# Attention and a feed-forward layer on one core: the sixth product of each output stage split into seven small ones

## The chip, the cores and the metric

The kernel runs on one core of a Trainium2 chip. The core has five engines that run side by side, each with its own queue of instructions in fixed order: TensorE (PE in the profile; PEld are its weight loads), VectorE (DVE), ScalarE (ACT), GpSimd (POOL) and SyncE (SP), which mostly issues transfers. TensorE writes into PSUM, eight banks of 512 float32 columns by 128 partitions; VectorE and ScalarE read it. The metric is device time of one execution in microseconds; lower is better.

## The reference

Eight batches of twelve heads, 448 tokens, head dimension 64. Softmax attention, then a layer with two weight matrices over all 3584 tokens, with a leaky ReLU between them:

```python
scores = scale * np.matmul(q, k.transpose(0, 1, 3, 2))
attn = np.exp(scores - max) / sum          # over the keys
x = np.matmul(attn, v)                     # to (3584, 768)
h = x @ w_in                               # (768, 2048)
g = np.maximum(0.01 * h, h)
out = g @ w_out                            # (2048, 768)
```

## The kernel before

Everything is written out by hand in one order per engine; the kernel keeps no scheduler of its own at run time, so an instruction that waits holds up all that stand behind it on its engine.

**Stages.** The tokens are cut at `cuts = [0, 640, 1152, 1664, 2176, 2688, 3072, 3584]` (line 41) into seven stages, 0 to 6. Each stage has a w_in stage (`head` and `neck` for stage 0, `hidden(i)`, line 523, after that), which makes h from x, and a w_out stage (`second(i)`, line 1134), which makes the output from h. Attention for later tokens is woven into the w_out stages: per head pair u a burst (three chunks of scores into three PSUM slots, then three exps on ScalarE), a tail (a fourth, half-sized chunk), and later rows (the weighted sum of v, divided on VectorE: a reciprocal at line 974 and a multiply at line 975), whose result x is turned by a transfer into `xT`. 48 head pairs in all.

**Fewer products.** Both matrix products are done by a scheme of Strassen's kind with seven products where eight would stand. In a w_in stage each group of seven products has 6 matmuls of 256 columns each (192 in the 384-token stage 5); two such groups run at a time, one on the two PSUM `banks`, one on two `slots`, so that a step of `hidden` has two such products, first that of the slots, then that of the banks (in the first half). A w_out stage takes two pairs of token blocks (c = 0 and 1; `spots(i)` says which) and forms for each, in `block_pair` (line 660), products of 8 matmuls with 384 columns on two banks, b and a, by turns: b, a, b, a (`early`), then b and a (`late`). After each one VectorE reads the bank into the output tiles `o1` and `o2` (`keep` copies, line 687; `join` adds, line 693). The sixth product, last of `late`, is `h[hi, one] x w_out[hi, right]` and goes into the right half of `o1`. The seventh is not formed there in stages 1 to 6: `deep(i)` (line 624) forms it for both pairs at once by a second level of the same scheme, seven products of 4 matmuls with 192 columns (line 645), one in every step of the first half of the next w_in stage, each followed by a VectorE addition of 192 columns (line 649). Its sums of h are made ahead by `deep_sums` (line 611), its sums of weights once by `mix_deep` (line 448), in w_out stage 1. In stage 6, which has no stage behind it, `deep` is interleaved with the second pair, and `closing` (line 728) ends the kernel with products cut in halves of 192 columns.

In stage 0 all seven products are formed directly, and the banks are swapped after each pair, seven being odd; in the other stages they are not swapped, six being even.

**The order of attention.** `second(i)` walks over the steps of `block_pair` (one step is two matmuls) and after each calls `place` (line 1071), a planner that keeps a model of its own: a clock `now` that a step moves on by 0.325, for each slot the time at which it comes free, and the time at which ScalarE is done. A burst is written when the three slots are due, a tail when the first slot is, rows when the exps of u are done and a slot is due. `plan` (line 1068) says how many bursts each stage writes; `cap` and `keen` say how far rows may run ahead. The assertion after the loop asks that all bursts of the plan were placed. If a tail is still owed when a w_in stage starts, the loop at line 1207 writes it ahead of the first product there:

```python
if owed_t and step == 0:
    tail()
```

**Buffers.** `xT` is a ring of twelve blocks of 128 tokens; a transposed batch of 448 tokens may run over its end, and `close_ring` (line 480) copies what ran over to the start (stage 2 alone). q, k and v are loaded two head pairs at a time from POOL's queue into `ld_pool`, two buffers each; a load may be written when `to[...]` says that the casts are far enough. Output tiles come from `o_pool`, three buffers.

Of the kernel before, what the change touches and what calls it, by code (L numbers as in the profile page):

```python
# [16 lines left out]
def kernel(  # L17
# [32 lines left out]
    ld_pool = ctx.enter_context(tc.tile_pool(name="ld", bufs=2))  # L50
    cast_pool = ctx.enter_context(tc.tile_pool(name="cast", bufs=1))
# [7 lines left out]
    o_pool = ctx.enter_context(tc.tile_pool(name="o", bufs=3))  # L59
# [43 lines left out]
    NX = 12 * P  # L103

    def place_of(t):
        return (t - cuts[5]) % NX

    OVER = max(-t % S for t in cuts if place_of(t) == 0)
# [8 lines left out]
    deep_mix = w_pool.tile([P, 3, QH, QW], BF16)  # L117
    KEEP = 4
# [20 lines left out]
    for _ in range(3):  # L139
        rooms.append(o_pool.tile([P, DM], F32, name="o").bitcast(BF16)[:, :4 * NSC * D])  # L140
# [306 lines left out]

    def mix_deep():

        t, (t2, t3, t4) = w_mix[:, 2], (deep_mix[:, x] for x in range(3))  # L450
        lo, hi, left, right = slice(0, QH), slice(QH, MH), slice(0, QW), slice(QW, NW)
        sub, add = nc.vector.tensor_sub, nc.vector.tensor_add
        for by, o, x, y in (
            (sub, t3, t[:, hi, right], t[:, lo, right]),
            (add, t2, t3, t[:, lo, left]),
            (sub, t4, t[:, hi, left], t2),
            (sub, t[:, lo, right], t[:, lo, right], t[:, lo, left]),
        ):
            by(o, x, y)
            yield  # L460
# [19 lines left out]
    def close_ring(i):  # L480

        if place_of(cuts[i]) == 0 and cuts[i] % S:
            for hp in range(KD):
                nc.vector.tensor_copy(xT[:, hp, :OVER], xT_flat[:, (hp + 1) * NX:(hp + 1) * NX + OVER])
                yield
# [37 lines left out]
    def hidden(i):  # L523
# [63 lines left out]
        more = deep(i - 1) if i > 1 else None  # L587
        for r in range(2):
            ms = [4 * r, 4 * r + 2]
            todo = [group(chains[x], ms[x]) for x in range(2)]  # L590
            for step in range(7):
                for y in range(2):
# [5 lines left out]
                    if i > 1 and (r or step) and y == 1:  # L598
                        next(more, None)
# [11 lines left out]
    def deep_sums(i):  # L611

        one, two = (ts(x[1], P) for x in spots(i)[1])
        lo, hi = slice(MH, MH + QH), slice(MH + QH, MD)
        s3, s1 = h_mix[:, :QH, 0], h_mix[:, QH:, 0]
# [8 lines left out]
    def deep(i):  # L624

        one, two = (ts(x[1], P) for x in spots(i)[1])
        lo, hi = slice(MH, MH + QH), slice(MH + QH, MD)
        s3, s1 = h_mix[:, :QH, 0], h_mix[:, QH:, 0]
        t, (t2, t3, t4) = w_mix[:, 2], (deep_mix[:, x] for x in range(3))
        left, right = slice(0, QW), slice(QW, NW)  # L630
        o = [kept[i, c] for c in range(2)]
        end = i + 1 == NR
        taken = [slots.pop(0) for _ in range(2 if end else 1)]
        b, a = (x[:, 0, :QW] for x in taken) if end else (taken[0][:, x, :QW] for x in range(2))
        for ps, first, x, w, c, cols in (
# [7 lines left out]
        ):  # L643
            for m in range(QH):
                nc.tensor.matmul(ps, x[:, m], w[:, m], start=(first and m == 0), stop=(m == QH - 1), skip_group_check=True)  # L645
            if end and c and (ps is a or cols is left):
                nc.scalar.copy(o[c][:, cols], ps)
            else:
                nc.vector.tensor_add(o[c][:, cols], o[c][:, cols], ps)  # L649
            if ps is a and first and c == 0:  # L650
                nc.vector.tensor_sub(h[:, hi, one], h[:, hi, one], s1)
            if ps is a and not first:
                store(o[0], token(i, spots(i)[1][0][1]), slice(0, NW) if end else slice(0, DM))
            if w is t4:
                if not end:
                    store(o[1], token(i, spots(i)[1][1][1]))
                slots.extend(taken)
            yield

    def block_pair(i, c):  # L660
# [12 lines left out]
        kept[i, c] = o2  # L673
# [21 lines left out]
        def early():  # L695
# [7 lines left out]
            if last:  # L703
# [9 lines left out]
            keep(o2, right, a, calm)  # L713
            yield

        def late():
# [6 lines left out]
            yield  # L723
            yield from product(a, h[:, hi, one], w_out_sb[:, hi, right])
# [3 lines left out]
        def closing():  # L728

            both = (nc.sync, nc.scalar)  # L730
            yield from product(b, s3, t3)
            join(o2, left, b)
            idle(o2[:, right], b[:, :NW])
            store(o2, t0, left, both)
            yield
            cuts2 = [(ts(x, QW), slice(NW + x * QW, NW + (x + 1) * QW)) for x in range(2)]
            for (cols, at), ps, os in zip(cuts2, (a, slots[0][:, 0]), ((o1, o2), (o2, o1))):
                yield from product(ps, h[:, lo, two], t1[:, :, cols], first=True, cols=cols)
                for o in os:
# [12 lines left out]
        if last:  # L752
            more = deep(i)
            for x, _ in enumerate(early()):
                if x == 0:
                    next(parts[0])
                yield
# [5 lines left out]
            yield from closing()  # L763
            return
        if not c:
            parts[:] = [deep_sums(i)]
# [256 lines left out]
    def fetch(n=3):  # L1023
        if to["q"] == NPE:
            return
        for x, y in enumerate(("q", "cast", "v")):
            u = to["load"][x]
            if n and u <= ahead and (u <= FAR or u - 3 < to[y]):
# [39 lines left out]
    plan = [8, 6, 6, 6, 6, 4, 0]  # L1068
# [177 lines left out]
```

## Time and profile before

| | |
|---|---|
| median of 3 runs (lowest, highest) | 377.95 us (377.93, 378.19) |
| profiled execution: time, span | 378.34 us, 376.6 us |
| TensorE busy | 369.7 us, 98% |
| VectorE, ScalarE, POOL busy | 256.9, 259.6, 191.8 us |
| granted TensorE clock | 0.999 over the span |
| matmuls of 384 columns at line 682 | 326 ns mean a record |
| matmuls of 192 columns at line 645 | 246 ns a record, 168 of them |

A matmul's record is longer than its share of the stream, since matmuls overlap: what one costs is read from the distance of starts, or from the pieces of the chain. The same holds, less so, for VectorE, whose 0.55 us operations follow one another every 0.47 us.

### The profile page before, as it was taken

How to read it: one execution, taken by the hardware profiler on the slowest of the kernel's cores; microseconds unless marked ns; L12 is line 12 of the kernel's file. 1: busy time of each engine (PE TensorE's matmuls, PEld its weight loads, DVE VectorE, ACT ScalarE, POOL GpSimd, SP SyncE). 2: the span in 40 equal slices, each digit the busy share in tenths (PEclk: the TensorE clock that was granted, in tenths of full speed). 3: DMA queues.
4: the chain of work that ended last, by engine and by line, in shares of the span. 5: the costliest groups of instructions: out<-in, count | busy, mean ns of one | idle time of the engine just before them, and what ended most of it. 6: DMA issues, size and time to landing. Idle time of an engine off the chain costs nothing.

```text
span 376.6 us, 10120 instructions
## 1 busy us (share of the span) xinstructions
PE 369.7 (98%) x4008; PEld 265.7 (71%) x4008; DVE 256.9 (68%) x558; ACT 259.6 (69%) x399; POOL 191.8 (51%) x376
## 2 busy tenths in 40 slices
PE   7999999999999999999999999999999999999996
PEld 3664658756698556996569966599665995679765
DVE  4765858778666867766676665775847775685763
ACT  5997885866768776758766587666787668636721
POOL 7985871986268989624588235792347020000000
PEclk9999999999999999999999999999999999999999
DMA  9999999999499885973869648798455740321123
GB/s 155 200 203 207 191 204 201 156 159 164 93 178 143 114 163 87 197 158 60 157 121 148 144 64 86 170 147 167 61 66 98 143 110 0 79 58 45 42 65 105
DMA packets 99600, 48.08 MB, mean 128 GB/s; under 512 B 64608, under 2 KB 96352, under 8 KB 99552
## 3 DMA queue, kind: packets, MB, share of 16 engines
q0 software_dynamic: 39600, 22.47, 44.6%
q1 hardware_dynamic: 59504, 24.50, 32.6%
q8 instruction: 31, 0.51, 0.6%
q10 hardware_dynamic: 448, 0.47, 0.4%
q14 instruction: 17, 0.14, 0.1%
HBM read 45.61 MB, written 11.01 MB: 150 GB/s over the span
## 4 chain that ended last, share of the span: by engine, by line
PE 94%; DMA 2%; DVE 1%; issue 1%; POOL 1%; ACT 1%; POOLq 0%; ACTq 0%; DVEq 0%
PE g L682 30%; PE g L548 14%; PE sc L548 14%; PE sc L322 7%; PE sc L350 6%; PE g L424 4%; PE sc L319 4%; PE sc L645 4%; PE sc L362 3%; PE g L817 2%; PE sc L343 2%; DMA w_in_mix<-in_v_dram 2%; PE g L362 1%; PE g L301 1%; PE sc L424 1%
## 5 line engine op out<-in xcount | busy, mean ns | idle before, releaser
L331 ACT ACTIVATE e<-sc 128x896 bf16<-128x896 f32 (+1 forms) x144 | 123.6, 923 | 30.7 <-PE sc L322 20.8
L682 PE MATMUL g<-w_out_sb,h 128*128 128x384 bf16 (+1 forms) x440 | 84.1, 325 | 0.0
L682 PEld LDWEIGHTS <-h 128*128 128x128 bf16 x592 | 54.4, 98 | 41.4 <-issue 11.2
L537 ACT ACTIVATE h<-c 128x512 bf16<-128x512 f32 (+1 forms) x72 | 43.1, 610 | 30.2 <-DVE c L563 12.4
L548 PEld LDWEIGHTS <-w_in_sb 128*128 128x128 bf16 x576 | 54.6, 98 | 5.7
L190 POOL COPY qkb<-fq 112x512 bf16<-112x512 bf16 x34 | 23.9, 703 | 41.6 <-DMA qkT<-qkb 32.5
L548 PEld LDWEIGHTS <-w_in_mix 128*128 128x128 bf16 x432 | 40.5, 98 | 3.7
L201 POOL COPY v<-fv 128x384 bf16<-128x384 bf16 x30 | 18.5, 617 | 43.1 <-PE sc L350 40.7
L687 DVE COPY o<-g 128x384 f32<-128x384 f32 x47 | 26.0, 553 | 13.7 <-PE g L682 13.5
L350 PE MATMUL sc<-v,e 128*128 128x65 bf16 x720 | 33.3, 193 | 0.0
L322 PE MATMUL sc<-qkT 64*128 64x448 bf16 (+1 forms) x210 | 32.8, 352 | 0.0
L350 PEld LDWEIGHTS <-e 128*128 128x128 bf16 x720 | 31.1, 98 | 1.3
L974 DVE RECIPROCAL rec<-sc 112x8 f32<-112x8 f32 x42 | 8.7, 207 | 33.6 <-PE sc L350 19.1
L975 DVE TENSOR_TENSOR x<-sc,rec 112x512 bf16<-112x512 f32 x42 | 29.0, 691 | 1.6 <-DVE rec L974 0.2
L548 PE MATMUL g<-xT,w_in_sb 128*128 128x256 bf16 (+1 forms) x216 | 28.5, 268 | 0.0
L548 PE MATMUL sc<-xT,w_in_sb 128*128 128x256 bf16 (+1 forms) x216 | 28.5, 268 | 0.0
L693 DVE TENSOR_TENSOR o<-o,g 128x384 f32<-128x384 f32 x39 | 21.4, 549 | 9.1 <-PE g L682 4.4
L343 PE MATMUL sc<-v,e 128*128 128x130 bf16 x120 | 26.5, 221 | 0.0
L649 DVE TENSOR_TENSOR o<-o,sc 128x192 f32<-128x192 f32 x39 | 13.7, 351 | 17.9 <-PE sc L645 17.9
L682 PE MATMUL g<-w_mix,h 128*128 128x384 bf16 x128 | 24.6, 326 | 0.2 <-DVE o L687 0.2
L163 POOL DMA_DIRECT2D fv<-in_v_dram x32 | 20.1, 641 | 7.7 <-DMA fq<-in_q_dram 3.1
L682 PE MATMUL g<-w_mix,hmix 128*128 128x384 bf16 x112 | 21.7, 326 | 0.0
(149 smaller groups left out, 744.1 us busy)
## 6 DMA issues: line engine op xcount, KB each, us to landing
fq<-in_q_dram POOLq DMA_DIRECT2D x17, 224.0 KB, 5.7
w_out_sb<-in_moe_w_out_dram POOLq DMA_DIRECT2D x4, 768.0 KB, 13.2
out_dram<-o SPq DMA_DIRECT2D x7, 336.0 KB, 3.4
w_in_sb<-in_moe_w_in_dram POOLq DMA_DIRECT2D x2, 1152.0 KB, 12.7
out_dram<-o SPq DMA_DIRECT2D x7, 288.0 KB, 3.4
fk<-in_k_dram POOLq DMA_DIRECT2D x15, 128.0 KB, 5.9
fv<-in_v_dram POOLq DMA_DIRECT2D x15, 128.0 KB, 4.8
out_dram<-o SPq DMA_DIRECT2D x7, 240.0 KB, 3.1
```

The costliest lines, as they stand in the source:

```text
L163: nc.gpsimd.dma_start(out=t[p, :n, :, :so].rearrange("p u h so d -> p (u h) (so d)"), in_=(q, k, v)[x][b, hs, keys].rearrange("h (p so) d ...
L190: by(t[:SC, x].rearrange("p so h d -> p h so d"), f)
L322: nc.tensor.matmul(ps[:, j, :S].rearrange("p (so s) -> p so s", so=NSC), t[p, 1, c], t[p, 0, :, :SC], start=True, stop=True,)
L331: nc.scalar.activation(e[:, :, c, :], ps[:n, :, :S], AX.Exp, scale=scale)
L343: nc.tensor.matmul(ps, e[:, EM + qc * SC:EM + qc * SC + P], vt[:, 2 * KC:].rearrange("p j d -> p (j d)"), start=True, stop=False, skip_gro ...
L350: nc.tensor.matmul(ps[:, j * (D + 1):(j + 1) * (D + 1)], e[:, at:at + P], vt[:, j * KC + c], start=False, stop=(c == KC - 1), skip_group_c ...
L537: nc.scalar.activation(hs[:, m:m + 2, cols], x.rearrange("p (m t) -> p m t", m=2), AX.Prelu, alpha=0.01)
L548: nc.tensor.matmul(ps[:, j * nh:(j + 1) * nh], w[:, kk, ts(j, P)], x[:, kk], start=(first and j == 0 and kk == 0), stop=(kk == KH - 1), sk ...
L682: nc.tensor.matmul(ps[:, cols], x[:, m], w[:, m], start=(first and m == 0), stop=(m == MH - 1), skip_group_check=True,)
L687: by(o[:, at], ps[:, :NW])
L693: nc.vector.tensor_add(o[:, at], o[:, at], ps[:, :NW])
L975: nc.vector.tensor_mul(x, ps[:, :, :, :D], rec.to_broadcast([SC, 2, 2 * NP, D]))
```

## The change

The sixth product of each pair is no longer formed in `late` in stages 1 to 6 (the function returns after the fifth). The sixth products of both pairs together are formed as a second `deep`, side 0, with seven small products in the next w_in stage: in every step of its first half one small product of side 1 follows the banks' product, as before, and one of side 0 follows the slots' product. Side 0 uses the second banks of the two taken slots. Its weight sums go to a new tile `deep_mix6`, its h sums to the other half of `h_mix`, all three written at the end of the second pair. Both output tiles of a pair are kept until then, so `o_pool` has four buffers, and stores move with them. In the last stage side 0 is woven into `closing`. To make room, `xT` has nine blocks with stages placed one behind the other (`begin`), and `close_ring` now copies in stages 2, 4 and 6; v loads have one buffer (`ldv_pool`), and are written only when the casts before them are. The plan becomes 9, 6, 6, 6, 6, 3, 0.

```diff
-    o_pool = ctx.enter_context(tc.tile_pool(name="o", bufs=3))
+    o_pool = ctx.enter_context(tc.tile_pool(name="o", bufs=4))
...
-    NX = 12 * P
+    NX = 9 * P
+    begin = [0]
+    for i in range(1, NR):
+        t = begin[-1] + cuts[i] - cuts[i - 1]
+        begin.append(t if t + cuts[i + 1] - cuts[i] <= NX else 0)
+    over = [-cuts[i] % S if i and begin[i] == 0 else 0 for i in range(NR)]
...
-        if not rooms:
-            return ld_pool.tile([n, 2, NSC, D], F32, name="f" + "qkv"[x])
+        if not rooms and x == 2 and spare and spare.pop(0) is not None:
+            rooms.append(last_room)
+        if not rooms:
+            return (ldv_pool if x == 2 else ld_pool).tile([n, 2, NSC, D], F32, name="f" + "qkv"[x])
...
+    def deep_w(side):
+        t, d = (w_mix[:, 2], deep_mix) if side else (w_out_sb[:, MH:, NW:], deep_mix6)
+        return t, [d[:, x] for x in range(3)]
...
 def close_ring(i):
-        if place_of(cuts[i]) == 0 and cuts[i] % S:
+        if over[i]:
+            at = begin[i - 1] + cuts[i] - cuts[i - 1]
...
 def hidden(i):
-        more = deep(i - 1) if i > 1 else None
+        more, also = iter(()), iter(())
+        if i > 1:
+            more = deep(i - 1, 1, [slots[0][:, x, :QW] for x in range(2)])
+            also = deep(i - 1, 0, [x[:, 1, :QW] for x in taken])
...
-                    if i > 1 and (r or step) and y == 1:
-                        next(more, None)
+                    if r or step:
+                        next(more if y else also, None)
...
+    def deep_x(i, side):
+        x = h_mix[:, :, 1 - side]
+        if i + 1 == NR and not side:
+            x = x_mix.rearrange("p x k n -> p (x k n)")[:, :MH * P].rearrange("p (m t) -> p m t", t=P)
+        return x[:, :QH], x[:, QH:]
...
 def block_pair(i, c):
-        kept[i, c] = o2
+        kept[i, c] = o1, o2
...
             yield from product(a, h[:, lo, two], t1, first=True)
             keep(o2, right, a, calm)
+            if i:
+                join(o1, right, a)
             yield
         def late():
             yield from product(b, s3, t3)
             if i:
                 keep(o2, left, b, calm)
             join(o2, right, b)
...
             yield
+            if i:
+                return
             yield from product(a, h[:, hi, one], w_out_sb[:, hi, right])
...
-        def closing():
+        def closing(more):
-            yield from product(b, s3, t3)
+            for _ in product(b, s3, t3):
+                yield
+                next(more)
+                yield
...
-            for (cols, at), slot in zip(cuts2, slots[1:]):
-                ps = slot[:, 0]
-                yield from product(ps, h[:, hi, one], w_out_sb[:, hi, right][:, :, cols], first=True, cols=cols)
-                nc.vector.tensor_add(o1[:, at], o1[:, at], ps[:, cols])
-                store(o1, token(i, x1), at, both)
+                next(more)
+                yield
+            for _ in more:
                 yield
...
         for x, _ in enumerate(late()):
-            if i and not c and (x == 4 or x == 6 and i + 1 == NR):
-                next(parts[0])
+            if i and x == 3:
+                if c:
+                    for _ in deep_sums(i, 0):
+                        pass
+                else:
+                    next(parts[0])
+                    if i + 1 == NR:
+                        next(parts[0])
...
-            if u < NU and u - 3 < (to["cast"], to["cast"], to["v"])[x] and u - 4 < min(to["load"]):
+            if u < NU and u - (3 if x < 2 or u <= HY else 1) < (to["cast"], to["cast"], to["v"])[x] and u - 4 < min(to["load"]):
...
-    plan = [8, 6, 6, 6, 6, 4, 0]
+    plan = [9, 6, 6, 6, 6, 3, 0]
...
-                if c or x < 20 or not 0 < i < NR - 2:
-                    turn_next(i)
+                turn_next(i)
...
-                if i == 1 and not c and x > 2 and x % 4 == 2:
+                if i == 1 and x > 2 and x % 4 == 2:
                     next(deeps, None)
```

More of the change, by code (lines that the diff above doesn't have):

```diff
@@ L622, in deep_sums, with deep @@
             yield
-    def deep(i):
-        one, two = (ts(x[1], P) for x in spots(i)[1])
+    def deep(i, side, taken):
+        one, two = (ts(x[side], P) for x in spots(i)[1])
         lo, hi = slice(MH, MH + QH), slice(MH + QH, MD)
-        s3, s1 = h_mix[:, :QH, 0], h_mix[:, QH:, 0]
-        t, (t2, t3, t4) = w_mix[:, 2], (deep_mix[:, x] for x in range(3))
+        s3, s1 = deep_x(i, side)
+        t, (t2, t3, t4) = deep_w(side)
         left, right = slice(0, QW), slice(QW, NW)
-        o = [kept[i, c] for c in range(2)]
+        o = [kept[i, c][side] for c in range(2)]
         end = i + 1 == NR
-        taken = [slots.pop(0) for _ in range(2 if end else 1)]
-        b, a = (x[:, 0, :QW] for x in taken) if end else (taken[0][:, x, :QW] for x in range(2))
-        for ps, first, x, w, c, cols in (
+        b, a = taken
+        for n, (ps, first, x, w, c, cols) in enumerate((
             (b, True, h[:, lo, one], t[:, :QH, left], 0, left),
@@ L756, in block_pair @@
                     next(parts[0])
+                if x in (8, 9, 10):
+                    next(sums6)
                 yield
@@ L1027, in fetch @@
             u = to["load"][x]
-            if n and u <= ahead and (u <= FAR or u - 3 < to[y]):
+            if n and u <= ahead and (u <= FAR or u - (3 if x < 2 or u <= HY else 1) < to[y]):
                 load_soft(u, 2, (x,))
```

75 lines of the change are left out of this document (41 added, 34 removed).

## The prediction

> **What bounds the kernel now.** I read the page's first part, then the waits of TensorE, the busy times by stretch (one w_out or w_in stage each), the chain, and last the timeline at the places where the change moves something.
>
> ```profile
> PE 369.7 (98%) x4008; PEld 265.7 (71%) x4008; DVE 256.9 (68%) x558; ACT 259.6 (69%) x399; POOL 191.8 (51%) x376
> ...
> PE 94%; DMA 2%; DVE 1%; issue 1%; POOL 1%; ACT 1%; POOLq 0%; ACTq 0%; DVEq 0%
> ```
>
> The chain that ends last is TensorE for 94% of the span. The wait list of TensorE holds six entries, 3.0 us together, and one of 0.2 us among the w_out products:
>
> ```profile
> PE g L682 <- DVE o L687: 0.2, 1, 0.2
> ```
>
> So nothing else is late anywhere between 123 and 370 us: what TensorE streams is the time, and a wait that the change puts into its queue is added in full. By stretch (us, then busy PE, PEld, DVE, ACT, POOL), a w_out stage (first line), the next w_in stage, and the same pair one later:
>
> ```profile
> 170.74:196.16 25.42, 25.42 (x252) 14.75 (x250) 16.97 (x35) 19.41 (x27) 14.17 (x32) 1.00 0.63 111
> 196.16:218.83 22.67, 22.67 (x255) 20.77 (x253) 15.88 (x34) 14.48 (x26) 14.19 (x29) 1.00 0.84 142
> 218.83:244.25 25.42, 25.42 (x252) 14.81 (x250) 16.44 (x35) 19.39 (x27) 12.83 (x30) 1.00 0.68 109
> 244.25:266.90 22.65, 22.65 (x254) 20.76 (x252) 15.95 (x35) 14.46 (x26) 14.19 (x29) 1.00 0.84 142
> ```
>
> Prices of products, from the chain (start, length, what): six of 384 columns in 0.97 us are 162.5 ns each, eight of 192 in 0.66 us are 82.5 ns.
>
> ```profile
> 187.53 0.67 PE sc L322 x6
> 188.21 1.08 PE g L682 x6
> ...
> 282.73 0.97 PE g L682 x6
> ...
> 368.34 0.66 PE sc L645 x8
> ```
>
> Last, the seam from w_out stage 2 to w_in stage 3, where the fifth product (b) of the second pair is followed by the sixth (a):
>
> ```profile
> 193.56 1.46 PE L682 MATMUL g<-w_mix,hmix 128*128 128x384 bf16 x8
> ...
> 194.87 1.46 PE L682 MATMUL g<-w_out_sb,h 128*128 128x384 bf16 x8
> 195.07 0.56 DVE L687 COPY o<-g 128x384 f32<-128x384 f32 x1
> 195.54 0.54 DVE L693 TENSOR_TENSOR o<-o,g 128x384 f32<-128x384 f32 x1
> ...
> 196.16 0.82 PE L548 MATMUL sc<-xT,w_in_sb 128*128 128x256 bf16 x6
> ...
> 196.82 0.82 PE L548 MATMUL g<-xT,w_in_sb 128*128 128x256 bf16 x6
> ```
>
> VectorE frees bank b at 196.08, 1.21 us after the fifth product gave way at 194.87. Today the sixth product (1.3 us) covers that. The w_in stage needs bank b with its second product, 0.66 us after its start.
>
> **The change, part by part.**
>
> **Products.** In stages 1 to 5, 16 x 162.5 ns = 2.60 us go and 28 x 82.5 ns = 2.31 us come: 0.29 us less, 1.45 us in five stages. In stage 6 the second pair's sixth product is already cut into 16 of 192 columns: 1.30 + 1.32 - 2.31 = 0.31 us less. Sum **-1.76 us**. Against this speaks the Trainium skill, "TensorE: Matmul & The Clock Gate", Back-to-back issue gap: in a stream with weight loads it gives about 81 ns at 128 columns and 131 ns at 512. Interpolated, an estimate, that is 89 and 114 ns, the change would add about 3.5 us of products, and the sum below would be 389.2. The rows disagree: 82.5 and 162.5 ns in this stream.
>
> **A: the ninth burst of stage 0.** The plan moves a burst (scores of one head pair, three exps) from stage 5 to stage 0; its TensorE work only moves. In stage 0 the eighth burst stands at 98.49, 16 products before the end.
>
> ```profile
> 98.49 0.74 PE L322 MATMUL sc<-qkT 64*128 64x448 bf16 x6
> 98.95 2.54 ACT L331 ACTIVATE e<-sc 128x896 bf16<-128x896 f32 x3 [0.79 <-PE sc L322]
> ```
>
> By the planner's own numbers (no rows in between: the first slot is due 1.55 after a burst, the tail 0.43 after the third exp) the next burst fits seven steps later: the last step, two products before the end. Its tail is then still owed and is issued as the first thing of w_in stage 1, into the only slot left, which holds the third exp. Burst to end of the third exp is 3.00 us; TensorE has 0.67 + 0.33 us until it comes to the tail, and a released product starts 0.05 us after (125.63 + 0.55 against 126.23). **+2.05 us**. Bounds: 0, if the tail fits; 3.0, if ScalarE is late. I take the row.
>
> **B: five seams w_out to w_in.** With the sixth product gone the w_in stage begins right behind the fifth product. Bank b is free 1.26 us after (1.21 + 0.05), wanted after 0.66 us: 0.60 us in four seams; before the 384-token stage six products of 192 columns cover 0.49 us: 0.77. **+3.17 us**. Nothing else stands there: the planner's sixth burst comes at step 37 of 42 and its tail at step 40, before the end; rows are capped. Bounds: 0.3 and 1.2 us each (VectorE 0.6 us late, as behind a 0.69 us row multiply).
>
> **C: five seams between the pairs.** Same hand-over, but the planner's 42 steps put rows (1.03 us) and a tail (0.19 us) exactly there, step 21: 1.26 - 1.22, five times, **+0.2 us**; 0 to 1.5.
>
> **D: the seam between the pairs of stage 6**, with no attention left. There ScalarE and VectorE read bank b one after the other:
>
> ```profile
> 361.31 2.13 PE L682 MATMUL g<-w_out_sb,h 128*128 128x384 bf16 x12
> 361.51 0.48 ACT L687 COPY o<-g 128x384 f32<-128x384 f32 x1 [0.82 <-PE g L682]
> 362.02 0.55 DVE L693 TENSOR_TENSOR o<-o,g 128x384 f32<-128x384 f32 x1 [3.28 <-ACT o L687]
> ```
>
> 362.57 + 0.05 - 361.31 = **+1.31 us**; 0.8 at least, the addition alone.
>
> **E: VectorE in w_out stage 1.** It is busy 19.8 of 25.8 us there and gains four mixes of w_out (0.55 us each) and three sums (0.42 each), loses one row pass (0.90 us, moved to w_in stage 2), in a stretch 3.6 us shorter: 22.4 of about 22. Some lateness falls on the seam: **+0.5 us**; 0 to 1.5.
>
> **F: the closing.** The seven small products of side 0 end the kernel; each is followed by a VectorE addition (0.35 us), beside the four and the join that were there. Placing them in order, the last addition ends 0.92 us after the last product against 0.42 now: **+0.5 us**; 0 to 1.2. Two stores of 384 columns instead of 192 at the end: nothing, the landings are 2.0 and 2.2 us.
>
> **At nothing.** In each w_in stage VectorE gains seven additions (0.35) and one subtraction (0.42): 15.9 + 2.9 of 22.7 + 2.3 us, and every bank is read two steps (3.9 us) before it is written again; without that cover a product would wait some 0.5 us. Twelve ring copies of 0.25 us (stages 3 and 5, first pair) on VectorE, 16.4 of 25.4 us busy; uncovered, 3 us of VectorE in two stages. The ring itself: stage 2's places are stage 0's, whose head ended at 61 us, before row 12 at 70.1; no write waits. Loads of v with one buffer instead of two: a landing takes 4.8 us on POOL's queue, in front of casts of q and k; cast v stands four row passes (3.92 us each) ahead, 15.7 us; if this cover were gone, 4.8 us per pair of u. SP: transposes are allowed in four more steps a stage and stores move to the w_in stage, 3.1 us before a landing against 8 us until an o buffer is written again. Rows moved into w_in stages (1.03 us each) move TensorE time only.
>
> **Sum**: -1.76 + 2.05 + 3.17 + 0.2 + 1.31 + 0.5 + 0.5 = **+5.97 us**. It is made against the profiled execution: span 376.6, 378.34 with what lies around it. The median shown is 377.95, 0.39 less. I carry the difference to the median: 377.95 + 5.97 = **383.9 us**.
>
> **Rivals.** (1) Faster, one mechanism: TensorE has other work at the hand-overs, because the planner's order puts a burst, rows or a tail there and fits the ninth tail. Then A to D are gone, -1.76 + 1.0 = 377.2, or 376.2 if E and F are nothing too. It decides once less than 0.76 us of the 6.7 us of waits is left. For it: at the seam between pairs exactly this happens. Against it: caps and owed tail as worked out. 0.07; and 0.02 that it comes out within 0.2%, which is about what the times here can tell from no change. (2) Only the ninth tail fits: 381.9. The next step was missed by little (3.37 against 3.43), so the count is thin. 0.12. (3) VectorE becomes the bound of all shorter w_out stages (17.3 of 21.8 us even in stage 2, in order behind waits) and is 0.7 us later at each hand-over: five times, 387.4. 0.13. (4) The small products run at the pace of their weight loads, 98 ns a row: 28 x 98 = 2.74 against 2.60, 0.14 us more per stage instead of 0.29 less, 386.5. Eight in 0.66 us speak against it. 0.04. The page's rule named above is this rival with its own figures, 389.2. The forecast as summed: 0.62.
>
> **The numbers.** 383.9 is the likeliest. From rival 2 with some seams cheaper (379.5) to rival 3 (387.5) lies about 0.85. Faster 0.07, same 0.02, slower 0.91.
>
> **What would show it.** L682 falls by 104 products (80 in stages 1 to 5, 24 in stage 6) and L645 rises by 168. The busy times by stretch: w_out stage 2 about 21.8 us (2.60 less products, one row pass moved), w_in stage 3 about 26.6. TensorE's waits gain about five entries of L548 on VectorE's L693, 0.6 us each; one of L322 on L331, about 2 us; one of L682 on L693, 1.3 us. Wrong it would be if these entries are missing: then rival 1.

## The result and the profile after

The changed kernel takes 388.72 us (median of five runs, 388.42 to 390.24) against 377.95 in the same comparison (377.64 to 378.94): a ratio of 1.0288, interval 1.0263 to 1.0312. Forecast were 383.9 us, with about 0.85 for 379.5 to 387.5. Slower was right; 4.8 us of the 10.8 were not foreseen. The profiled executions differ by as much: 389.03 against 378.34 us, spans of 387.3 and 376.6.

In the changed kernel line 682 has become L707, L645 is L672 (small products), L649 is L677 (their additions), L693 is L718 (join), L687 is L712 (keep), L548 is L566 (products of a w_in stage), L322 and L331 are L334 and L343 (scores and exp). The page of the changed kernel, busy time by engine and then the chain that ended last:

```profile
PE 371.2 (96%) x4072; PEld 270.1 (70%) x4072; DVE 280.4 (72%) x638; ACT 258.9 (67%) x399; POOL 188.8 (49%) x376
...
PE 87%; DVE 8%; ACT 2%; issue 1%; DVEq 0%; ACTq 0%
```

TensorE's share of the chain fell from 94% to 87%, and VectorE, at 1% before, now holds 8% of it. The waits of TensorE (engine, line and tile; what released it; us in total, times, the longest) name the places:

```profile
PE g L566 <- DVE o L718: 2.8, 5, 0.9
PE sc L334 <- ACT e L343: 1.9, 1, 1.9
PE sc L566 <- DVE o L677: 1.7, 5, 0.7
...
PE g L707 <- DVE o L718: 1.2, 1, 1.2
```

The first, second and last of these lines are the three entries that the prediction named (B, A, D). The third is not in it. (The entry left out, 1.2 us at line 253, stands in the list of the kernel before too.) The busy times by stretch, w_out stage 2 and w_in stage 3 (stretch, length, busy PE, PEld, DVE, ACT, POOL, clock, DMA share, GB/s):

```profile
176.23:198.04 21.81, 21.81 (x207) 12.14 (x206) 14.46 (x31) 17.83 (x25) 11.41 (x26) 1.00 0.79 104
198.04:225.06 27.02, 26.45 (x311) 24.15 (x309) 21.33 (x48) 15.84 (x29) 15.06 (x31) 1.00 0.80 137
```

The w_out stage is the 21.8 us that were forecast, and TensorE is busy all of it. The w_in stage is 27.0 instead of 26.6. What happens at its beginning shows in the first 8 us of this stage alone, the kernel before first, the changed one second:

```profile
196.16:204.16 8.00, 8.00 (x80) 7.31 (x78) 5.42 (x13) 4.56 (x8) 7.82 (x16) 1.00 0.89 144
```
```profile
198.04:206.04 8.00, 7.43 (x72) 6.56 (x71) 7.20 (x18) 5.06 (x9) 2.98 (x7) 1.00 0.94 121
```

VectorE went from 5.42 to 7.20 us of work in 8. The timeline there (start, length, engine, line, operation; in brackets the idle time before it and its releaser):

```profile
198.04 0.82 PE L566 MATMUL sc<-xT,w_in_sb 128*128 128x256 bf16 x6
198.17 0.56 DVE L712 COPY o<-g 128x384 f32<-128x384 f32 x1 [1.25 <-PE g L707]
198.64 0.55 DVE L718 TENSOR_TENSOR o<-o,g 128x384 f32<-128x384 f32 x1
...
199.10 0.42 DVE L649 TENSOR_TENSOR hmix<-h 128x512 bf16<-128x512 bf16 x1
199.24 0.81 PE L566 MATMUL g<-xT,w_in_sb 128*128 128x256 bf16 x6 [0.39 <-DVE o L718]
...
199.56 0.42 DVE L649 TENSOR_TENSOR h<-h 128x512 bf16<-128x512 bf16 x1
...
200.02 0.42 DVE L649 TENSOR_TENSOR hmix<-h 128x512 bf16<-128x512 bf16 x1
...
200.36 0.28 DVE L517 TENSOR_TENSOR x_mix<-xT 128x256 bf16<-128x256 bf16 x1
...
201.21 0.68 DVE L581 TENSOR_TENSOR c<-c,sc 128x512 f32<-128x512 f32 x1
...
201.81 0.35 DVE L677 TENSOR_TENSOR o<-o,sc 128x192 f32<-128x192 f32 x1
...
202.21 0.81 PE L566 MATMUL sc<-x_mix,w_in_mix 128*128 128x256 bf16 x6 [0.18 <-DVE o L677]
```

Two things are late. The products on bank b (tile g) start at 199.24, 0.05 us after the join has read it: term B. From the keep at 198.17 on VectorE then has no gap: join, side 0's three sums of h, three mixes of x (line 517), the addition of line 581, and only then the first small addition of side 0, which ends at 202.16. The slots' third product (tile sc, from `x_mix` and `w_in_mix`) starts at 202.21, 0.05 us after that end, although the addition read the other bank of that slot.

To count what is lost at a place I take the distance from one product's start to the next one's, less its own price (162.5 ns with 384 columns, 109 with 256, 82.5 with 192). At places that lose over 0.23 us, in us, over the five seams where there are five:

| place | lost | term |
|---|---|---|
| owed tail at the start of w_in stage 1 | 2.04 | A, 2.05 |
| bank b behind the join | 0.80, 0.55, 0.55, 0.71, 1.04 = 3.65 | B, 3.17, and part of E |
| slots' product behind the first small addition ("second wait") | 0.87, 0.35, 0.35, 0.59, 0.35 = 2.51 | none; "at nothing" |
| between the pairs of stages 1 to 5 | none over 0.23 | C, 0.2 |
| between the pairs of stage 6 | 1.32 | D, 1.31 |
| closing: three waits of small products | 0.38 + 0.25 + 0.24 = 0.87 | F, 0.5 |
| closing: last matmul's start to the end of the span | 5.34 against 3.81, +1.53 | F |

With -1.76 for the products this is +10.2; the span grew by 10.7, and the 0.5 us left over, by difference, lie in gaps too small for the table.

### The profile page after: what moved, and what is told of

It is laid out like the page before. It is cut to its first block, busy times and chain, and to the rows that moved or that the text cites. A ratio compares the mean times of both kernels' runs of the same rounds, so it can differ in the third digit from the quotient of the medians.

```text
span 387.3 us, 10362 instructions
## 1 busy us (share of the span) xinstructions
PE 371.2 (96%) x4072; PEld 270.1 (70%) x4072; DVE 280.4 (72%) x638; ACT 258.9 (67%) x399; POOL 188.8 (49%) x376
## 4 chain that ended last, share of the span: by engine, by line
PE 87%; DVE 8%; ACT 2%; issue 1%; DVEq 0%; ACTq 0%
PE g L707 23%; PE g L566 13%; PE sc L566 13%; PE sc L334 6%; PE sc L672 6%; PE sc L362 6%; PE sc L331 4%; PE g L436 4%; PE sc L374 3%; PE g L859 2%; ACT e L343 2%; PE sc L355 2%; PE g L313 1%; PE g L374 1%; DVE o L718 1%
## 5 line engine op out<-in xcount | busy, mean ns | idle before, releaser
L343 ACT ACTIVATE e<-sc 128x896 bf16<-128x896 f32 (+1 forms) x144 | 123.9, 928 | 28.0 <-PE sc L334 17.9
L707 PEld LDWEIGHTS <-h 128*128 128x128 bf16 x488 | 44.9, 98 | 36.0 <-issue 11.2
L707 PE MATMUL g<-w_out_sb,h 128*128 128x384 bf16 (+1 forms) x352 | 66.2, 325 | 1.2 <-DVE o L718 1.2
L566 PEld LDWEIGHTS <-w_in_sb 128*128 128x128 bf16 x576 | 54.1, 98 | 11.3 <-issue 5.8
L566 PEld LDWEIGHTS <-w_in_mix 128*128 128x128 bf16 x432 | 40.4, 98 | 5.8 <-issue 2.4
L213 POOL COPY v<-fv 128x384 bf16<-128x384 bf16 x30 | 15.4, 515 | 53.9 <-issue 21.7
L677 DVE TENSOR_TENSOR o<-o,sc 128x192 f32<-128x192 f32 x78 | 27.3, 350 | 17.1 <-PE sc L672 16.9
L334 PE MATMUL sc<-qkT 64*128 64x448 bf16 (+1 forms) x210 | 32.9, 352 | 1.9 <-ACT e L343 1.9
L712 DVE COPY o<-g 128x384 f32<-128x384 f32 x47 | 25.9, 551 | 11.6 <-PE g L707 9.9
L566 PE MATMUL g<-xT,w_in_sb 128*128 128x256 bf16 (+1 forms) x216 | 28.5, 268 | 2.8 <-DVE o L718 2.8
L566 PE MATMUL sc<-xT,w_in_sb 128*128 128x256 bf16 (+1 forms) x216 | 28.5, 268 | 0.0
L707 PE MATMUL g<-w_mix,h 128*128 128x384 bf16 x128 | 24.8, 327 | 0.0
L718 DVE TENSOR_TENSOR o<-o,g 128x384 f32<-128x384 f32 x39 | 21.3, 546 | 4.8 <-ACT o L712 2.6
L672 PEld LDWEIGHTS <-h 128*128 128x128 bf16 x240 | 21.4, 98 | 2.6 <-issue 0.9
L707 PE MATMUL g<-w_mix,hmix 128*128 128x384 bf16 x112 | 22.9, 327 | 0.0
```

Source lines behind the costliest of these rows:

```text
L334: nc.tensor.matmul(ps[:, j, :S].rearrange("p (so s) -> p so s", so=NSC), t[p, 1, c], t[p, 0, :, :SC], start=True, stop=True,)
L343: nc.scalar.activation(e[:, :, c, :], ps[:n, :, :S], AX.Exp, scale=scale)
L566: nc.tensor.matmul(ps[:, j * nh:(j + 1) * nh], w[:, kk, ts(j, P)], x[:, kk], start=(first and j == 0 and kk == 0), stop=(kk == KH - 1), sk ...
L677: nc.vector.tensor_add(o[c][:, at], o[c][:, at], ps)
L707: nc.tensor.matmul(ps[:, cols], x[:, m], w[:, m], start=(first and m == 0), stop=(m == MH - 1), skip_group_check=True,)
L712: by(o[:, at], ps[:, :NW])
```

## The experiments

Three theories of the seams. **Theory 1**: the wait for bank b and the second wait stand for themselves. **Theory 2**: VectorE is late from the seam on; whoever waits for it first is the one listed, and one wait taken away lengthens the next. **Theory 3**: the slot is read too late in any case, whatever stands ahead. All runs below but the ring alone go against 388.72 us; differences between places are read from profiled executions. None of these kernels leaves out work.

### The banks exchanged

```diff
             yield
             if i:
+                banks.reverse()
                 return
```

> The changed kernel with the two banks of a pair exchanged at the end of each pair after stage 0, so that the next stage's first product begins in the bank that came free earlier (a), not in the one just filled (b). Against 388.7 us. Theory 1, each wait stands for itself: the waits of the first product on the join (2.8 us in five w_out to w_in seams, 1.2 us in stage 6) go, and with them about 5 us: 383.7. Theory 2, VectorE's backlog sets the end of the seam: VectorE works from 198.17 to 202.16 without a gap, and the slots' second product waits for the end of it in any case, so what the bank gives is added to that second wait (now 1.7 us in five, it would come to about 4.5); only stage 6's 1.3 us is kept: 387.3. Both: the wait on the join goes from the list.

Measured 387.76 us (387.25 to 389.57). The wait on the join is gone, and the other has grown from 1.7 to 4.4 us:

```profile
PE sc L566 <- DVE o L677: 4.4, 5, 1.2
```

At the second wait 1.14 + 0.90 + 0.64 + 1.17 + 1.39 = 5.24 us are lost, where both places together lost 6.16. Five seams freed give 0.9 us, and stage 6 gives 1.0 (1.32 lost before, 0.28 now), of which some small places elsewhere take part back. The time lies at theory 2's 387.3 and far from theory 1's 383.7: theory 1 is out.

### The owed tail later

```diff
-            if owed_t and step == 0:
+            if owed_t and step == (4 if i == 1 else 0):
...
-    ... (step > 16 or i == 1):
+    ... (step > 16 or i == 1 and step > 2):
```

> The changed kernel with the ninth burst's owed tail written at step 4 of w_in stage 1 rather than at step 0, and the stage's three rows moved to steps 6, 10 and 14. Against 388.7 us. If term A is the lateness of that tail as the prediction says (a 1.9 us wait of the score product on the exp, 2.04 us lost between 102.7 and 104.9), it goes: 386.7, and that wait is gone from the list. If ScalarE is simply behind at that place (the rows, not the tail's place), the wait comes back further on in the same stage and the time stays within 0.4 us of 388.7.

Measured 386.87 us (386.70 to 387.28), -1.85. The 1.9 us entry is gone; in its place the first product of w_in stage 1 waits a little for the same exp's slot (0.42 us lost):

```profile
PE sc L566 <- ACT e L343: 0.3, 1, 0.3
```

The first of the second waits also fell, from 0.87 to 0.35, because the whole seam came 1.5 us earlier, and its mixes of x were done before a cast on GpSimd began (last section). Of term A the place is shown, and the size: 2.04 us less the 0.42 that is left there, and the 0.52 of the later seam, make the 2.1 us by which the profiled span fell.

### Side 0's sums behind the first small addition

```diff
-                if c:
-                    for _ in deep_sums(i, 0):
-                        pass
...
                         next(more if y else also, None)
+                    if i > 1 and r == 0 and step == 1 and y:
+                        for _ in deep_sums(i - 1, 0):
+                            pass
```

> The changed kernel with side 0's three sums of h (half a microsecond each, 1.35 us in all) taken out of the last steps of each w_out stage and put into step 1 of the following w_in stage, behind the first small addition. Banks as in the changed kernel. Against 388.7 us. Theory 2 (the slots' second product waits for the backlog that these sums make up): the second wait (1.7 us in five, 2.51 us lost) goes, the first one on the join stays at 2.8 us: 386.2. Theory 3 (the second wait is the slot's bank itself, read by the small addition half a microsecond after it is filled, whatever stands ahead of it): 388.3 or more, and the wait stays near 1.7 us.

Measured 390.39 us (389.12 to 391.80): slower. Theory 2's 386.2 is missed; the time lies in theory 3's open range (388.3 or more), but the wait that theory 3 asks for is not there. The second wait as it was is gone; the three sums now stand ahead of the third small addition, and the slots' next product waits for that one:

```profile
201.78 0.82 PE L566 MATMUL sc<-x_mix,w_in_mix 128*128 128x256 bf16 x6
...
203.80 0.61 DVE L652 TENSOR_TENSOR hmix<-h 128x512 bf16<-128x512 bf16 x1
...
204.33 0.34 DVE L680 TENSOR_TENSOR o<-o,sc 128x192 f32<-128x192 f32 x1
...
204.72 0.82 PE L566 MATMUL sc<-xT,w_in_sb 128*128 128x256 bf16 x6 [0.81 <-DVE o L680]
```

The product at 201.78 has no wait any more: theory 3 is out. But 1.35 us of sums in one go find no room in the first three steps, and at both places tried they delay a slot's reader. Lost there: 3.27 instead of 2.51 us. Another 0.65 us came at the end of the span, which this edit does not touch.

### Banks and sums together

> Both edits at once: the banks exchanged and side 0's sums later. Against 388.7 us. Theory 1 (waits stand for themselves): the sum of the two single gains, whatever these are. Theory 2 (one backlog behind both waits): the banks' gain is far larger here than alone; B (3.65), the second wait (2.51) and stage 6's 1.3 us all go, 381.3 us, at most 382.5 if the mixing of x still makes the second product wait some 0.2 us a stage.

Measured 386.36 us (385.79 to 387.43). Behind the moved sums the banks give 4.0 us (390.39 to 386.36) where alone they gave 1.0, as theory 2 has it. The forecast of 381.3 is missed by 5 us. Of these, 3.50 are lost at the wait that the sums' new place brings (2.7 us in the list); the rest lies in places of less than half a microsecond each.

### The sums on GpSimd, with the banks as they are and exchanged

```diff
-            (nc.vector.tensor_sub, s3, h[:, lo, one], h[:, lo, two]),
+            (eng.tensor_sub, s3, h[:, lo, one], h[:, lo, two]),
...
+        eng = nc.vector if side or i + 1 == NR else nc.gpsimd
```

> The changed kernel with side 0's three sums of h (stages 1 to 5) done by GpSimd in place of VectorE, in the same place; GpSimd stands idle from 197.7 to 202.8 there, and the sums are first read by the third small product, at 204.8. Banks as in the changed kernel. Against 388.7 us. Theory 2 (VectorE's backlog: 1.35 us of sums ahead of the addition that the slots' second product waits for): that wait (1.7 us in five, 2.51 us lost) goes, the wait on the join stays at 2.8 us: 386.2. Theory 3 (the slot is simply filled too late to be read in time): the wait stays: 388.3 or more. A third outcome, three sums that are slow on GpSimd and late for the third small product, would show as a wait of small products on GpSimd: up to 1 us a stage, 390 or more.

> The banks exchanged at the end of each pair, and side 0's sums on GpSimd. Against 388.7 us. If the wait on the join and the second wait have one cause between them (VectorE late from the seam on), the banks alone gave 1.0 and should give the rest here: B 3.65 + second wait 2.51 + stage 6's 1.32, in all 7.5: 381.2, between 380.8 and 382.5. If another VectorE wait takes their place (the small additions and the c11 additions of step 1 come to 2.06 us in a step of 1.97), some 0.4 us a stage comes back: 383.3.

Measured 394.60 us (392.66 to 395.15) and 389.05 us (388.79 to 389.45). The first lies where the third outcome put it (390 or more), but without its sign: no small product waits for GpSimd. The second is far from its forecasts. The sums were not late; VectorE was. Timeline of the first of the two:

```profile
198.54 1.15 POOL L650 TENSOR_TENSOR h<-h 128x512 bf16<-128x512 bf16 x1
198.88 0.62 ACT L578 COPY c<-sc 128x512 f32<-128x512 f32 x1
198.89 0.95 DVE L517 TENSOR_TENSOR x_mix<-xT 128x256 bf16<-128x256 bf16 x1
...
199.77 1.15 POOL L650 TENSOR_TENSOR hmix<-h 128x512 bf16<-128x512 bf16 x1
199.88 1.19 DVE L517 TENSOR_TENSOR xT<-xT 128x256 bf16<-128x256 bf16 x1
...
201.10 0.29 DVE L517 TENSOR_TENSOR x_mix<-xT 128x256 bf16<-128x256 bf16 x1
```

The mixes of x take 0.95 and 1.19 us beside a sum on GpSimd, 0.29 once GpSimd is done. So VectorE's queue was no shorter, and the runs say nothing against theory 2. They also don't test it as was meant. In the last seam of the first run two mixes, of 1.34 and 1.26 us, stand ahead of the keep, and bank b loses 2.80 us where it lost 1.04; behind that wait the granted clock fell as well, to 0.50 from 344 to 346 us (last section).

### Stage 6 as before

```diff
-            if i:
+            if 0 < i < NR - 1:
                 return
...
-            yield from closing(deep(i, 0, [x[:, 0, :QW] for x in slots[1:]]))
+            yield from closing()
```

(with the old `closing`, and in w_in stage 6 one VectorE addition that puts back the quarter of w_out)

> The changed kernel with w_out stage 6 as in the kernel before: its sixth product formed directly, no side 0 there, and the old closing (the quarter of w_out that is mixed in place is added back by VectorE in w_in stage 6). Against 388.7 us. If D (1.32 us) and the closing (0.86 us of waits and 1.7 us from the last product to the end, about 2.5 against a term F of 0.5) are what stage 6 lost, less the 0.3 us that its small products saved: 385.2. If F was right at 0.5 and the rest of the end is the place of the last stores whatever the products are: 387.2.

Measured 387.69 us (385.79 to 388.58), beside the second forecast, 387.2; the two fastest executions, 385.79 and 385.98, lie nearer the first, 385.2. The profiled execution is the lowest, 3.2 less than the changed kernel's. In it the 1.32 between the pairs and the 0.87 of closing waits are gone, and from the last matmul's start to the end are 4.03 us instead of 5.34. So the places are shown; the size (3.2 us in the profiled executions, 1.0 by the medians) is less sure.

### The two slots of side 0 exchanged

```diff
-            also = deep(i - 1, 0, [x[:, 1, :QW] for x in taken])
+            also = deep(i - 1, 0, [x[:, 1, :QW] for x in taken[::-1]])
```

> The changed kernel with the two taken slots of side 0 exchanged: its small products of even number then go beside the slots' chain's odd steps. Both banks of a slot are one tile. If a product waits for readers of the whole tile, not of its bank, the first small product of side 0 has to wait for the c11 addition of the same slot (it ends at 201.9 where the product now starts at 200.6): about 1.3 us more in each of five stages, less the present second wait of 0.5: 392.7, between 391 and 395, with small products waiting for VectorE's L581. If waits go by the bank, nothing that the products wait for is changed: 388.7 within 0.5.

Measured 419.05 us (418.40 to 419.72). Not one small product a stage waits but six, each for a reader of the other bank of its slot:

```profile
PE sc L672 <- DVE c L581: 6.6, 5, 1.5
PE sc L672 <- DVE c L596: 3.8, 5, 0.8
PE sc L672 <- DVE c L593: 3.8, 5, 0.8
PE sc L672 <- ACT h L555: 3.3, 5, 0.7
PE sc L672 <- ACT c L586: 3.3, 5, 0.7
PE sc L672 <- ACT c L590: 3.3, 5, 0.7
```

Of a taken slot, lines 555 and 581 to 596 read only bank 0; the small products write only bank 1. So the waits go by the whole tile. The direction was forecast, the size (391 to 395) not: I had counted one wait a stage where there are six.

### The ring alone

The kernel before with the nine-block ring, its copies, the own buffer for v and the fourth output buffer, and no second level.

> The kernel before with the nine-block ring alone (its ring copies, the v loads with one buffer of their own, the fourth output buffer), no second level for the sixth product. Against 377.95 us. The prediction put the ring, its copies and the later v loads at nothing: 377.95 within 0.4. If the ring or the loads cost something that the changed kernel's account hides in another term: 378.5 to 380, with SP, GpSimd or DMA as the releaser of a new wait.

Measured 377.93 us against 378.17 in the same comparison, ratio 0.9996 (0.9977 to 1.0015); no entry in the list of waits with SP, GpSimd or DMA as its releaser. The ring costs nothing beyond that interval.

### The sums parted

```diff
+            if i and c and x == 11:
+                sums0[:] = [deep_sums(i, 0)]
+                next(sums0[0])            # h lo two += h hi two, in the w_out stage
...
+                    if i > 1 and r == 0 and (step, y) in ((1, 1), (4, 1)):
+                        next(sums0[0])    # s1 in step 1; s3 = h hi two - s1 in step 4
```

(The comments in the last cut are not in the kernel.)

> The changed kernel with side 0's three sums parted (stages 1 to 5): the addition early in the pair's own w_out stage, s1 behind the two additions of step 1, and s3 in step 4, formed as (second half of h) minus s1, which is the same sum. So VectorE has 1.35 us less ahead of the slots' second product, and no step gets more than one sum. Banks as in the changed kernel. Against 388.7 us. Theory 2 (VectorE's queue between the seam and that product is the cause of the second wait): it goes, 2.51 us lost become 0.3 or less, and the wait on the join stays at 2.8 us: 386.3. If the additions of step 1 alone are too late (2.06 us of them in 1.97): the wait stays above 1 us: 387.5 to 388.7.

> The sums parted, and the banks exchanged. Against 388.7 us. Theory 2 (one late VectorE queue behind both waits, so that the bank pays only when the queue is short): B 3.65, second wait 2.51 and stage 6's 1.32 all go: 381.2; if the mixes of x that still stand there make the second product wait 0.3 us a stage: 382.7. Theory 1 (separate waits): the single gains add, 1.0 for the banks and 2.4 for the sums: 385.3.

Measured 391.69 us (390.05 to 392.00) and, with the banks exchanged, 386.96 (385.86 to 387.73). Theory 2's 386.3 and 381.2 to 382.7 are missed by more than 4 us. The second run lies nearer theory 1's 385.3, but not by its account: the wait on the join is gone there too, and what is over lies elsewhere. The second wait is gone in both (0.41 and 0.23 us are left in two stages of the second run). But s3 in step 4 is one step ahead of its reader, and late: small products lose 3.5 and 3.4 us behind it. Timeline of the first:

```profile
210.00 0.35 DVE L683 TENSOR_TENSOR o<-o,sc 128x192 f32<-128x192 f32 x1
...
210.26 0.42 DVE L655 TENSOR_TENSOR hmix<-h,hmix 128x512 bf16<-128x512 bf16 x1
...
210.74 0.51 PE L678 MATMUL sc<-deep_mix,hmix 128*128 128x192 bf16 x4 [0.47 <-DVE hmix L655]
```

Without the exchange B also grew, from 3.65 to 4.89 (1.76 in the first seam, 1.32 in the last), where VectorE has the addition more to do ahead of the join.

### The same with s3 one step earlier

`(4, 1)` becomes `(3, 1)`.

> The banks exchanged and the sums parted as before, with s3 one step earlier (step 3, where VectorE has 0.7 us free, in place of step 4). Against the profiled 385.86 of the run with s3 in step 4: if s3's lateness was all of its new wait (small products on VectorE's sum, 0.63 to 0.87 us in five stages, 3.4 us lost), 382.5 profiled, 382 to 383.5 as a median; that wait is gone from the list. If VectorE is full in step 3 as well, the wait goes to the chain's products or stays: 384 or more.

Measured 384.05 us (383.63 to 385.16), above the 382 to 383.5 that were expected; profiled 383.63, 1.1 above the forecast. The wait on s3 is gone, and of 6.16 us at the two waits 0.63 is left. What is over is no wait. The row of granted clock has one slice of forty below 9 tenths:

```profile
PEclk9999999999989999999999999999999999999999
```

Closer up (stretch, length, busy PE, PEld, DVE, ACT, POOL, clock, DMA share, GB/s), right behind the 2.04 us wait for the owed tail:

```profile
104.00:106.00 2.00, 1.44 (x8) 0.99 (x8) 0.12 (x1) 1.05 (x2) 2.00 (x4) 0.70 1.13 169
106.00:108.00 2.00, 2.00 (x19) 1.63 (x18) 0.00 (x0) 1.06 (x2) 0.66 (x2) 0.50 1.11 135
108.00:110.00 2.00, 2.00 (x33) 1.86 (x31) 1.03 (x3) 0.12 (x1) 1.11 (x4) 0.95 1.31 278
```

Matmuls of 256 columns follow each other every 213 ns there instead of 109. By these three clocks some 1.7 us of TensorE's work went (an estimate: 0.30, 0.50 and 0.05 of 2 us each), more than the 1.1 that are over. The other three executions show a lower mean clock as well (0.993 to 0.995).

### All mended

The tail apart, the banks exchanged, the sums parted and stage 6 as before, first with s3 in step 4, then with s3 in step 3 and the banks of stage 6 left alone.

> All that the runs so far named, at once: tail apart (A), banks exchanged (B), sums parted (second wait), and stage 6 as in the kernel before (D and the closing). Against 388.7 us. If these are the places where the time went: 388.7 - 2.04 - 3.65 - 2.51 - 3.24 (the profiled gain of stage 6 as before) = 377.3 us, beside 377.95 of the kernel before; 378.8 if 0.3 us a stage is left at the second product. If something else of the change costs time that these places only show (the clock, the weight loads, DMA), it stays above 380.

Measured 383.75 us (382.99 to 384.00), neither 377.3 nor 378.8, but above the 380 that was to mean a cause left out. Two waits of my own making stood in it: s3 (3.19 us lost) and, with the sixth product direct again, the exchanged bank between the pairs of stage 6 (1.28).

> All mended, with s3 in step 3 and the banks left as they are in stage 6. Against the profiled 382.99 of the first such run: 3.2 us (s3) and 1.28 us (the pair seam of stage 6) less: 378.5 profiled, within 0.6; beside the kernel before, 377.95, no faster, since five stages of small products save only 1.5 us and 0.8 us of waits and some small gaps are left. If it stays above 381, the account lacks a cause.

Measured 379.26 us (378.70 to 380.76), profiled 378.74: forecast 378.5 within 0.6. The list of TensorE's waits has nothing left among the w_out and w_in stages but these two:

```profile
PE sc L566 <- ACT e L343: 0.3, 1, 0.3
...
PE sc L566 <- DVE o L686: 0.2, 1, 0.2
```

So the five places (A, B, the second wait, D and F) are where the time went. Against the kernel before the ratio is 1.0032 (1.0011 to 1.0053), 0.1 to 0.5% slower, with the same profiled span, 376.6 us: with 1.45 us of products saved, 0.83 us lost at the two places left, and 0.8 in small gaps, there was nothing to win.

## Why the prediction was wrong

**Products** (-1.76): L707 runs 600 matmuls where L682 ran 704, L672 336 where L645 ran 168, as said; eight small ones pass in 0.66 us. The rate that the Trainium skill states in "TensorE: Matmul & The Clock Gate", Back-to-back issue gap, would, by the prediction's estimate, have made the small products dearer and the large ones cheaper, and its sum, 389.2, lies beside the measured 388.7. That is chance: w_out stage 2 takes 21.81 us, all of it busy, where the rows gave 21.8. The time was lost in waits.

**A, C, D** were right: 2.04 for 2.05, nothing for 0.2, 1.32 for 1.31. **B** was right in its mechanism, in the two plain seams (0.55 for 0.60 each) and before the 384-token stage (0.71 for 0.77); the first (0.80) and the last (1.04) lost more, within its upper bound. In the last a mix of x stands on VectorE ahead of the keep (338.13 to 338.55). **E** (0.5) is at most the 0.25 that B's first seam lost more than the plain ones.

**"At nothing", VectorE in the w_in stages, is the step that failed** (2.51 us; F, below, is a second one, a term too small by 1.9). It had two parts, and both were wrong.

- "Every bank is read two steps (3.9 us) before it is written again." Banks, yes; but here a wait goes by the slot, which is a tile of two banks. The first small product of side 0 is written beside the slots' chain half a step ahead of the next product on the same tile. The cover was therefore the distance from 201.04, where that small product ends, to 201.87, where the next one on the slot is due, 0.8 us, and not 3.9. Shown by the exchanged slots, 30 us slower.
- "15.9 + 2.9 of 22.7 + 2.3 us" is an average over the stage. In its first 8 us, which were 5.42 us full and are now 7.20, stand the keep of bank b, side 0's three sums, two more additions and one more subtraction than before. The sums are not among what the prediction counted for the w_in stages: they stand behind the join on VectorE, and so run there (199.10 to 200.44 in the timeline). Shown by the exchanged banks alone (5.24 us lost at the second wait) against the same with the sums parted (0.63 left).

The price that the prediction put beside it, should the cover be gone ("some 0.5 us"), is the mean of what was measured, 2.51 us over five seams, 0.35 to 0.87 each. It was not carried into the sum or into a rival. Rival 3's 387.4 is nearer the result, but not by its mechanism: it put VectorE's lateness into the w_out stages and at the hand-over, while w_out stage 2 ran without a wait and the lateness came behind the hand-over.

**F** (+0.5) is 2.4. The additions were placed nearly right: the last one ends 0.95 us after the last matmul's start where it was 0.64, 0.3 us more. Two things were not in it: small products that wait for the addition before them (0.87), and "two stores of 384 columns instead of 192: nothing". The stores of o and e stand behind each other on both queues:

```profile
382.25 0.35 DVE L677 TENSOR_TENSOR o<-o,sc 128x192 f32<-128x192 f32 x1
...
382.51 0.35 DVE L677 TENSOR_TENSOR e<-e,sc 128x192 f32<-128x192 f32 x1
382.80 0.47 SPq L414 DMA_DIRECT2D out_dram<-o  x1
382.87 0.54 ACTq L414 DMA_DIRECT2D out_dram<-o  x1
383.37 0.55 SPq L414 DMA_DIRECT2D out_dram<-e  x1
383.51 0.68 ACTq L414 DMA_DIRECT2D out_dram<-e  x1
```

The last issue ends at 384.19, 1.3 us after the last addition; in the kernel before the last addition ends at 373.40 and the last issue at 373.80. The end of the span follows 3.1 and 2.8 us after. That it belongs to the new end is shown: from the last matmul's start to the end of the span the eleven profiled executions with it take 5.28 to 5.99 us, the five with the old one 3.79 to 4.03. That it is the order of the two stores was read from this timeline and not tried by itself.

**Ring, copies, loads of v** at nothing: shown in the order of the kernel before (0.9996). In the changed order three of the runs (stage 6 as before, and the two under "The sums parted") have a wait of 0.3 to 0.5 us of TensorE on a cast of v; the changed kernel has none.

The difference of 4.8 us (4.7 by the spans), term by term: second wait 2.51, F 1.90 more, B 0.48 more, small gaps 0.5, less E (0.5) and C (0.2), which were in the sum and have no loss of their own. That these two were too large hid 0.7 us of what was missing, by luck.

## What to carry to other kernels

Price added work on a side engine by how full its first microseconds behind a hand-over are, not by the stage's average: 18.8 of 25.0 us seemed to leave room, 7.2 of the first 8 left none, and one sum of 0.42 us a stage, placed a step earlier, was worth 2.9 us (386.96 to 384.05). Ask of each buffer what unit a wait is kept for; two banks in one tile wait for each other's readers. And where two engines' waits stand in a row, removing the first shows little until the engine behind both is relieved: 1.0 us alone, 4.0 and 4.7 with the sums elsewhere.

## What the runs showed of the hardware

VectorE and GpSimd get in each other's way. A VectorE sum of two SBUF operands (L517, 128x256 bfloat16), 0.28 us by itself, took 0.95 to 1.19 us beside a GpSimd sum of 1.15 us, and one of 512 columns 1.34; keeps and joins with one operand in PSUM took 0.56 and 0.55 as ever. The Trainium skill, "SBUF — State Buffer", SBUF: two separate sides, states that the two share a port pair under an exclusive lock, held for a whole instruction, when the VectorE instruction has two SBUF inputs and the GpSimd instruction reads SBUF; the rows agree: the two slow sums end at 199.84 and 201.07, each 0.15 us after the GpSimd sum beside it. The changed kernel has the same once, at the seam from w_out stage 1 to w_in stage 2, with mere casts on GpSimd:

```profile
151.20 0.61 POOL L202 COPY qkb<-fq 112x512 bf16<-112x512 bf16 x1 [3.31 <-DMA qkT<-qkb]
151.76 0.56 POOL L206 COPY qkb<-fk 128x384 bf16<-128x384 bf16 x1
```
```profile
151.32 0.63 DVE L517 TENSOR_TENSOR xT<-xT 128x256 bf16<-128x256 bf16 x1
...
151.99 0.47 DVE L517 TENSOR_TENSOR x_mix<-xT 128x256 bf16<-128x256 bf16 x1
```

These two mixes took 0.63 and 0.47 us instead of 0.29, and the second wait of that seam is 0.52 longer than that of the next. Where the mixes ran at another time than the casts (tail apart, stage 6 as before), it is 0.35. What took 0.42 us on VectorE took 1.15 us on GpSimd, and held up VectorE for most of that.

A long wait of TensorE can cost more than itself. Behind the 2.04 us for the owed tail in the run with s3 in step 3, and behind the 2.80 us in the last seam of the first run with sums on GpSimd, the granted clock read 0.50 for a while (106 to 108 and 344 to 346 us) and was 1.00 again by 110 and 348 us. It does not always come: in the profiled execution of the changed kernel, with the same 2.04 us, it read 1.00 from 104 to 110 us. What decides it, these runs do not show.
